# Attention output in token order: one store per output tile, the last product in two column halves, one product held back

## The chip, the cores and the metric

The kernel runs on one core of one Trainium2 chip. The metric is the device time of one execution in microseconds; the time of a kernel is the median of several executions.

## The reference

Softmax attention over 8 batches of 12 heads, 448 tokens and 64 dimensions per head, followed by a two-layer block with a SiLU between its layers. All tensors are float32.

```python
scores = np.matmul(q, k.transpose(0, 1, 3, 2)) / sqrt(64)     # q, k, v: (8, 12, 448, 64)
attn = softmax(scores)
attn_out = np.matmul(attn, v)
x = attn_out.transpose(0, 2, 1, 3).reshape(8 * 448, 12 * 64)  # (3584, 768)
h = x @ w_in                                                  # w_in:  (768, 2048)
g = h / (1 + np.exp(-h))
out = g @ w_out                                               # w_out: (2048, 768), out: (3584, 768)
```

## The kernel before

**Attention.** The work is cut into 24 units, one for each batch and group of four heads; a unit takes all 448 tokens. The queries of a unit are loaded so that partition 32 * head + i holds the 14 neighbouring tokens 14 * i to 14 * i + 13 (`group_of`, `TPP` is 14). After the 32 x 32 transposes (`turn_k`, `turn_q`) column 32 * g + i of a unit stands for token 14 * i + g. So the scores, their exponentials (`expo`, L442, on ScalarE), the products with V (`attend`, L479) and all that follows have their columns in the order "g i" and not in token order. Two exponentials of a unit are added on VectorE (`add_e`, L453) into T; sums of T and E over the keys are products with ones (L495, L515). `inverse` transposes the sums, takes the reciprocals (L554) and transposes them back (L546, L560) into `rdn`.

**The normalisation.** `norm` (L576) takes the product with V from a PSUM bank, multiplies it by 0.5 and by `rdn`, and writes one of the six 128 x 448 fp16 slices of `xT` of its batch. It runs twice per unit, 48 times in all. It frees the PSUM bank that the product stood in.

**The two layers.** The first layer (`ffn1`, L394, or `pair_product`, L729, for two batches together) multiplies slices of `w_in` by `xT` and leaves h / 2 in a PSUM bank. `tanh` (L602) and `gate` (L640), or ScalarE's SiLU (L755), make the gated values `G` (and `X` for columns that lie over), with the columns in the order of `xT`. The second layer works on "quads": two row tiles of 128 columns of G, and two halves of 384 output columns, done with seven products instead of eight by combining operands (`combine_g` makes the sums `S`, L779; `combine_w` the differences `D` of the weights, L627). A quad's products run in the order 1, 5, 6, 2, 7, 3, 4. Each is eight matmuls of 384 columns (`product`). Three PSUM banks serve a quad: products 1 and 2 add up in the first, 6, 7 and 4 in the second, 5 and 3 in the third. Between them VectorE adds copies of banks into banks (`add_in`, L840: "u", then "w", which products 7 and 3 wait for), and `add_out` (L845) and `take_out` (L836, on ScalarE) write the four 128 x 384 float32 output tiles `ost`, of which four buffers exist. There are 14 quads, 0 to 13.

**The stores.** Because the columns are in the order "g i", 32 neighbouring rows of an output tile are 32 rows of the output that stand 14 rows apart. `store` (L825) therefore sends each tile with four DMAs of 32 rows, all from SyncE (SP), but for the last two quads, where ScalarE (ACT) issues every second one.

**What sets the order.** The order of all instructions is written out by a planner inside the kernel. `Order` keeps an assumed clock and, for each engine, the operations that may run; each `Op` has an assumed duration, what it depends on and a bias. The planner gives `norm` the duration 448 / 960 + 0.13 us. `Ring` objects hand out the buffers and banks by their assumed times of release. Nothing of it runs on the chip: there every engine takes its instructions in the order that the planner wrote down, and waits on semaphores.

Of the kernel before, what the change touches and what calls it, by code (L numbers as in the profile page):

```python
# [17 lines left out]
PE_OUT = 0.20  # L18
# [12 lines left out]
def mm(n):  # L31
    return n / 2400.0 + 0.0026


def act(n):
    return n * 0.00087 + 0.13
# [151 lines left out]
def kernel(  # L188
# [9 lines left out]
    nc = tc.nc  # L198

    B, NH, S, D = q.shape  # L200
# [4 lines left out]
    TPP = S // 32  # L205
# [9 lines left out]
    NT = 2 * S // 128  # L215
    OH = DM // 2
# [33 lines left out]
    def bank_m(*key):  # L250
        return bank_of(4 + spot[key])
# [45 lines left out]
    rawk, rawq, KT, QT, E, T, acc, rdn_t, xT, g_t, ost_t = ({} for _ in range(11))  # L297
# [92 lines left out]
    def wide(out, lhsT, rhs, **flags):  # L390
        n = 4 if od.strips else 1
        for j in range(n):
            at = slice(128 // n * j, 128 // n * (j + 1))
            nc.tensor.matmul(out=out[at], lhsT=lhsT[:, at], rhs=rhs, **flags)  # L394
# [169 lines left out]
    def x3(b, cc):  # L564
        if (b, cc // 3) not in xT:
            xT[(b, cc // 3)] = sb.tile(
                [128, 3, S], FP16, name=f"xT_{b}_{cc // 3}", tag="xT", bufs=NX3
            )
        return xT[(b, cc // 3)]

    def norm(n, part):
        b, hg, g0, g1 = units[n]
        nq = 32 * (g1 - g0)
        cc = 2 * hg + part - 1
        x3(b, cc)
        nc.vector.scalar_tensor_tensor(  # L576
            out=x3(b, cc)[:, cc % 3, 32 * g0 : 32 * g1],
            in0=acc[(n, part)][:, 0:nq],
            scalar=0.5,
            in1=rdn_t[n].rearrange("p g i -> p (g i)"),  # L580
            op0=ALU.mult,
            op1=ALU.mult,
        )
# [25 lines left out]
    HF = NFF // 2  # L609
    G = const.tile([128, NFF, 2 * S], FP16, name="G")  # L610
    X = const.tile([128, NFF, 128], FP16, name="X")
    W_ = {m: const.tile([128, HF, OH], FP16, name=f"D{m}") for m in (5, 6, 4)}
# [36 lines left out]
    def rows(t, i):  # L649

        fs = slice(HF * i, HF * (i + 1))
        u, k = divmod(t, NT)
        if u % 2 == 0 and k == NT - 1:
            return X[:, fs]
        return G[:, fs, 128 * k : 128 * (k + 1)]
# [106 lines left out]
    S_t, tmp_t, ost_t, pr_t = {}, {}, {}, {}  # L762
# [17 lines left out]

    BANK = {1: 1, 2: 1, 6: 6, 7: 6, 4: 6, 5: 5, 3: 5}

    def product(qd, m, f0, f1):
        a, b = 2 * qd, 2 * qd + 1
        if m in (5, 6):
            w = S_t[(qd, m - 4)]
        else:
            t, i = {1: (a, 0), 2: (a, 1), 3: (a, 1), 7: (b, 0), 4: (b, 1)}[m]
            w = rows(t, i)
        if BANK[m] == m and f0 == 0:  # L790
            pr_t[(qd, m)] = bank_m("p", qd, m)
        for f in range(f0, f1):
            wide(
                out=pr_t[(qd, BANK[m])][:, 0:OH],
                lhsT=w[:, f, :],
                rhs=W_[m][:, f, :],
                start=(f == 0 and BANK[m] == m),
                stop=(f == HF - 1),
                skip_group_check=True,
            )  # L800


    def bank(qd, m):
        return pr_t[(qd, m)][:, 0:OH]
# [5 lines left out]
    def ost(qd, i, j):  # L810
        t = sb.tile([128, OH], FP32, name=f"ost_{qd}_{i}{j}", tag="ost", bufs=NOST)
        ost_t[(qd, i, j)] = t
        return t

    def store(qd, i, j):
        u, t = divmod(2 * qd + i, NT)
        for w in range(4):
            r, col = divmod(128 * t + 32 * w, S)
            b = 2 * u + r
            dst = out[b * S : (b + 1) * S, OH * j : OH * (j + 1)].rearrange(  # L820
                "(i g) m -> g i m", g=TPP
            )

            eng = nc.scalar if w % 2 and 4 * qd + 8 >= NT * B else nc.sync
            eng.dma_start(  # L825
                out=dst[col // 32], in_=ost_t[(qd, i, j)][32 * w : 32 * (w + 1), :]
            )

    def take(qd, m):
        nc.scalar.copy(out=tmp(qd, m), in_=bank(qd, m))  # L830

    def take_out(qd, m, i, j):
        if m == 6 and qd == NT * B // 4 - 1:
            nc.vector.tensor_copy(out=ost(qd, i, j), in_=bank(qd, m))
        else:
            nc.scalar.copy(out=ost(qd, i, j), in_=bank(qd, m))  # L836
        store(qd, i, j)

    def add_in(qd, to, x, y):
        nc.vector.tensor_tensor(  # L840
# [16 lines left out]
    units = []  # L857
# [5 lines left out]
    od = Order(SHY)  # L863
# [68 lines left out]
    for n in range(NB0 + NG, NU):  # L932
        b, hg = units[n][:2]
# [47 lines left out]
    pr_op, sg_op, w_op = {}, {}, {1: [], 2: [], 3: []}  # L981
# [5 lines left out]
    def in_parts(n, size, columns, emit, done, at=0):  # L987
        to = min(at + size, n)
        op = Op("PE", (to - at) * mm(columns), lambda: emit(at, to), tail=PE_OUT)
        od.on_pe(op, "full")  # L990
        if to == n:
            done(op)
        else:
            moe.insert(
                0, (list, 0, lambda: in_parts(n, size, columns, emit, done, to), ())
            )
# [264 lines left out]
    def queue_quad(qd):  # L1261
        quads.append(qd)
        fourth.append(qd)
        took = {}

        def read(name, eng, fn, deps, then=None):
            busy = act(OH) if eng == "ACT" else OH / 960.0 + 0.13
            bias = B_TAKE if eng == "ACT" else B_READ
            took[name] = od.add(Op(eng, busy, fn, deps, bias, then=then))

        def out(m):
            def then(at):
                m_ring.give(at, spot[("p", qd, m)])
                ost_ring.give(at + STORE)

            return then

        def queue(m):
            def run():
                if BANK[m] == m:  # L1280
                    spot[("p", qd, m)] = m_ring.take()[0]
                for ring, need in rings:
                    ring.take(need)
                in_parts(HF, PROD_AT, OH, lambda f0, f1: product(qd, m, f0, f1), done)

            def done(op):
                if m == 5:
                    sg_ring.give(od.free["PE"] + PE_OUT)
                pr_op[(qd, m)] = op
                if m in (1, 5):  # L1290
                    read(m, "ACT", lambda: take(qd, m), [op])
                elif m == 6:
                    read("u", "DVE", lambda: add_in(qd, 6, 6, 1), [op, took[1]], tmp_ring.give)
                    read("w", "DVE", lambda: add_in(qd, 5, 6, 5), [took["u"], took[5]])
                elif m == 2:
                    read("11", "ACT", lambda: take_out(qd, 1, 0, 0), [op], out(1))
                elif m == 7:
                    read(
                        "22",
                        "DVE",  # L1300
                        lambda: add_out(qd, 6, 5, 1, 1),
                        [op],
                        lambda at: (ost_ring.give(at + STORE), tmp_ring.give(at)),
                    )
                elif m == 3:
                    read("12", "ACT", lambda: take_out(qd, 5, 0, 1), [op], out(5))
                else:
                    eng = "DVE" if qd == NT * B // 4 - 1 else "ACT"
                    read("21", eng, lambda: take_out(qd, 6, 1, 0), [op], out(6))

            def deps():
                made = list(w_op.get(m, [None]))
                made += [took.get(x) for x in {2: (1,), 7: ("w",), 3: ("w",), 4: ("22",)}.get(m, ())]
                first = {5: 1, 6: 5, 7: 6, 3: 7, 4: 3}.get(m)
                if first:
                    made.append((pr_op.get((qd, first)), 9.0))
                elif m == 1 and qd > 0:
                    made.append((pr_op.get((qd - 1, 1)), 9.0))
                if m in (1, 2, 4):
                    t = 2 * qd + (m == 4)  # L1320
                    for b in {(128 * t + c) // S for c in (0, 127)}:
                        for f in range(HF):
                            x = g_op.get((b, f + HF * (m > 1)), [None])
                            made += [(y, f * mm(OH)) for y in x]
                    return made + ld_wout
                x = sg_op.get((qd, {5: 1, 6: 2, 7: 3, 3: 4}[m]), [])
                x = x if len(x) == 2 else [None, None]
                return made + [x[0], (x[1], 4 * mm(OH))]

            rings = ((tmp_ring, 1),) if m in (1, 5) else ((ost_ring, 1),) * (m != 6)  # L1330
            moe.append((deps, int(BANK[m] == m), run, rings))

        for m in (1, 5, 6, 2, 7, 3, 4):
            queue(m)
# [300 lines left out]
    while True:  # L1635
# [49 lines left out]
        if warm["on"] and at is not None and od.free["PE"] <= od.now and wait > 0.06 and od.now > 0.9:  # L1685
            each = mm(128) if od.now > COLD else 0.07 if od.now > 6.5 else 0.107
            n = max(1, int((wait - 0.06) / each), int(wait / each + 0.9) * (od.now < 14.0))
            n += MORE0 * (6.5 < od.now < COLD) + 2 * (COLD < od.now < 14.0)
            if warm.pop("first", None):
                n = FIRST  # L1690
# [36 lines left out]
```

## Time and profile before

| what | value |
|---|---|
| median of 3 runs | 382.66 us (382.15 to 384.31) |
| the profiled execution's own time | 382.59 us |
| its span in the profile | 380.5 us |
| granted TensorE clock | 0.998 |
| PE busy | 373.6 us, 98% |
| DVE busy | 280.1 us, 74% |
| ACT busy | 254.4 us, 67% |
| `norm`, L576 | 48 times, mean 616 ns |
| stores | 208 from SP, 16 from ACT, 48 KB each, median 1.6 us (SP) and 1.8 us (ACT) to landing |

The profile shows one execution. PE is TensorE's matmuls, PEld its weight loads, DVE VectorE, ACT ScalarE, POOL GpSimd, SP SyncE. "L576" is line 576 of the kernel. A group of instructions is listed with its output and inputs, its count, its busy time and the mean of one, and then the idle time of the engine just before them with what ended it. The chain of waits goes back from the last instruction through whatever released each step. All times in the views are microseconds from the start of the span, unless marked ns.

### The profile page before, as it was taken

The numbers are of one execution on the slowest core, as the hardware profiler recorded it, in microseconds if no ns is written. First come the engines' busy times: TensorE is split into PE (matmuls) and PEld (weight loads), VectorE is DVE, ScalarE is ACT, GpSimd is POOL, SyncE is SP. The second block draws the span as 40 slices with busy tenths as digits, with TensorE's granted clock in tenths as the row PEclk, the third lists the DMA queues.
The fourth block names the chain that finished last, engine by engine and source line by source line (L and its number), as shares of the span: only waits on it lengthen the run. The fifth ranks groups of instructions, "written<-read, shape, count | busy, mean of one in ns | idle before, by whom it ended". The sixth has DMA issues, their size and how long they took to land.

```text
span 380.5 us, 12915 instructions
## 1 busy us (share of the span) xinstructions
PE 373.6 (98%) x5508; PEld 191.6 (50%) x5508; DVE 280.1 (74%) x560; ACT 254.4 (67%) x408; POOL 85.2 (22%) x155
## 2 busy tenths in 40 slices
PE   7999999999999999999999999999999999999995
PEld 6433455444455444444444454555556555556563
DVE  4689799999996868997869978789866334556333
ACT  4998864787867787967788787728762258772221
POOL 7537616406042603324240500000000000000000
PEclk9999999999999999999999999999999999999999
DMA  6999999936558843739491612120002330001333
GB/s 102 195 207 181 191 210 205 155 73 90 70 102 134 146 67 42 107 72 167 82 150 26 92 24 73 33 55 0 1 2 68 84 98 2 0 1 39 104 93 99
DMA packets 36009, 34.66 MB, mean 91 GB/s; under 512 B 12144, under 2 KB 35184, under 8 KB 35952
## 3 DMA queue, kind: packets, MB, share of 16 engines
q0 software_dynamic: 25200, 22.82, 40.5%
q1 hardware_dynamic: 9984, 10.24, 10.0%
q10 hardware_dynamic: 768, 0.79, 0.8%
q8 instruction: 43, 0.70, 0.8%
q14 instruction: 14, 0.11, 0.1%
HBM read 45.61 MB, written 11.01 MB: 149 GB/s over the span
## 4 chain that ended last, share of the span: by engine, by line
PE 93%; ACT 2%; DMA 2%; DVE 1%; issue 1%; POOL 0%; ACTq 0%; DVEq 0%; POOLq 0%
PE banks L394 55%; PE banks L729 15%; PE banks L404 11%; PE banks L479 10%; ACT E L442 2%; PE banks L495 2%; DMA rq<-in_q_dram 1%; PE banks L1626 0%; DMA out_dram<-ost 0%; DVE banks L840 0%; POOL rk L309 0%; DVE T L453 0%; PE banks L515 0%; DVE rq L387 0%; DVE ost L845 0%
## 5 line engine op out<-in xcount | busy, mean ns | idle before, releaser
L442 ACT ACTIVATE E<-banks 128x896 f16<-128x896 f32 x168 | 144.1, 919 | 41.4 <-PE banks L404 41.1
L394 PE MATMUL banks<-xT,w_in_t 128*32 128x448 f16 (+1 forms) x1446 | 90.5, 353 | 0.0
L394 PE MATMUL banks<-w_out_t,G 128*32 128x384 f16 (+1 forms) x1000 | 72.8, 327 | 0.1
L394 PEld LDWEIGHTS <-G 128*32 128x32 f16 (+1 forms) x1280 | 50.8, 97 | 36.9 <-issue 6.8
L394 PEld LDWEIGHTS <-w_in_t 128*32 128x32 f16 (+1 forms) x1446 | 42.2, 97 | 43.2 <-issue 12.7
L340 POOL DMA_DIRECT2D V<-in_v_dram x84 | 46.0, 560 | 55.2 <-PE banks L479 42.9
L404 PE MATMUL banks<-rq,KT 32*128 32x448 f16 (+1 forms) x768 | 52.1, 362 | 1.6 <-DVE rq L387 1.3
L602 ACT ACTIVATE th<-banks 128x448 f16<-128x448 f32 x72 | 37.2, 553 | 15.0 <-PE banks L394 13.2
L640 DVE SCALAR_TENSOR_TENSOR G<-th,banks 128x448 f16<-128x448 f16 (+1 forms) x72 | 39.8, 571 | 4.9 <-ACT th L602 4.5
L836 ACT COPY ost<-banks 128x384 f32<-128x384 f32 x41 | 19.6, 482 | 33.7 <-PE banks L394 18.2
L394 PE MATMUL banks<-D,S 128*32 128x384 f16 (+1 forms) x560 | 40.9, 327 | 0.0
L479 PE MATMUL banks<-E,V 128*32 128x448 f16 x672 | 35.7, 353 | 0.0
L755 ACT ACTIVATE G<-banks 128x448 f16<-128x448 f32 (+1 forms) x56 | 29.1, 525 | 6.5 <-DVE banks L745 3.5
L576 DVE SCALAR_TENSOR_TENSOR xT<-banks,rdn 128x448 f16<-128x448 f32 x48 | 29.1, 616 | 5.4 <-PE banks L479 2.8
L394 PEld LDWEIGHTS <-S 128*32 128x32 f16 (+1 forms) x560 | 22.2, 97 | 15.7 <-issue 3.1
L745 DVE TENSOR_TENSOR banks<-banks,q 128x448 f32<-128x448 f32 x28 | 17.6, 632 | 16.6 <-PE banks L729 15.4
L404 PEld LDWEIGHTS <-KT 32*128 32x128 f16 (+1 forms) x768 | 12.5, 96 | 30.8 <-issue 27.4
L453 DVE TENSOR_TENSOR T<-E,E 128x1792 f16<-128x1792 f16 x22 | 23.7, 1078 | 5.6 <-ACT E L442 5.5
L453 DVE TENSOR_TENSOR T<-T,E 128x1792 f16<-128x1792 f16 x22 | 23.8, 1083 | 5.2 <-ACT E L442 5.2
L317 POOL DMA_DIRECT2D rq<-in_q_dram x25 | 14.0, 559 | 59.0 <-PE banks L404 48.0
L479 PEld LDWEIGHTS <-V 128*32 128x32 f16 x672 | 17.0, 97 | 16.0 <-issue 4.3
L729 PEld LDWEIGHTS <-w_in_t 128*128 128x128 f16 x168 | 16.4, 98 | 15.2
(150 smaller groups left out, 386.0 us busy)
## 6 DMA issues: line engine op xcount, KB each, us to landing
out_dram<-ost SPq DMA_DIRECT2D x208, 48.0 KB, 1.6
rk<-in_k_dram POOLq DMA_DIRECT2D x23, 224.0 KB, 5.3
rq<-in_q_dram POOLq DMA_DIRECT2D x23, 224.0 KB, 5.4
w_out_t<-in_moe_w_out_dram POOLq DMA_DIRECT2D x4, 768.0 KB, 12.9
V<-in_v_dram POOLq DMA_DIRECT2D x42, 64.0 KB, 4.2
V<-in_v_dram POOLq DMA_DIRECT2D x42, 48.0 KB, 4.5
w_in_t<-in_moe_w_in_dram POOLq DMA_DIRECT2D x3, 512.0 KB, 11.3
w_in_t<-in_moe_w_in_dram POOLq DMA_DIRECT2D x6, 256.0 KB, 6.3
```

The costliest lines, as they stand in the source:

```text
L340: nc.gpsimd.dma_start(out=v_of(b, hg0)[32 * x : 32 * (x + 1), at, 0:count, :], in_=v[b, hs].rearrange("h (i g) d -> i h g d", g=TPP)[:, :, ...
L394: nc.tensor.matmul(out=out[at], lhsT=lhsT[:, at], rhs=rhs, **flags)
L404: nc.tensor.matmul(out=pS[p0 : p0 + 32 * (x1 - x0), h % 2, at : at + nq], lhsT=KT[(b, hg)][32 * h : 32 * (h + 1), c, x0:x1, :, e], rhs=QT[ ...
L442: nc.scalar.activation(out=E[(n, w)][0:kr, 2 * y : 2 * y + 2, 0:nk], in_=pS_t[(n, w, y)][0:kr, :, 0:nk], func=AF.Exp, scale=attn_scale,)
L453: nc.vector.tensor_tensor(out=T[n], in0=T[n] if step else E[(n, 0)], in1=E[(n, step + 1)], op=ALU.add,)
L479: nc.tensor.matmul(out=a[32 * h : 32 * (h + 1), 0:nq], lhsT=w, rhs=e[k0:k1, h, at : at + nq], start=start, stop=stop,)
L576: nc.vector.scalar_tensor_tensor(out=x3(b, cc)[:, cc % 3, 32 * g0 : 32 * g1], in0=acc[(n, part)][:, 0:nq], scalar=0.5, in1=rdn_t[n].rearra ...
L602: nc.scalar.activation(out=th, in_=h_t[(b, f, t0)][:, 0 : t1 - t0], func=AF.Tanh)
L640: nc.vector.scalar_tensor_tensor(out=dst[:, f, at + lo : at + hi], in0=th_t[(b, f, t0)][:, lo - t0 : hi - t0], scalar=1.0, in1=h_t[(b, f, ...
L729: nc.tensor.matmul(out=pp_t[(f, PBANK[m])], lhsT=w[:, c, :], rhs=a[:, c, :], start=(c == 0 and m in (1, 6, 5)), stop=(c == 2), skip_group_ ...
L755: nc.scalar.activation(out=dst[:, f, at + lo : at + hi], in_=pp_t[(f % HF, x)][:, lo:hi], func=AF.Silu, scale=2.0,)
L836: nc.scalar.copy(out=ost(qd, i, j), in_=bank(qd, m))
```

## The change

- `norm` writes `xT` in token order: it reads the bank and `rdn` in the order "g i" as before, and writes the element of column 32 * g + i to column 14 * i + g. The elements are fp16, so that elements written one after the other lie 28 bytes apart. Nothing between `xT` and the output cares for the order of the columns.
- A tile of output is then 128 neighbouring rows, and `store` is one DMA of 128 rows x 384 columns, 192 KB, from SP.
- The very last product (quad 13, product 4) is made in two halves of 192 columns, eight matmuls each; DVE copies the first half out and SP stores it, ACT copies and stores the second.
- Quad 12's product 4 is held back until quad 13's product 6 has been queued.

```diff
     def norm(n, part):
-        b, hg, g0, g1 = units[n]
-        nq = 32 * (g1 - g0)
+        b, hg = units[n][:2]
         cc = 2 * hg + part - 1
         x3(b, cc)
         nc.vector.scalar_tensor_tensor(
-            out=x3(b, cc)[:, cc % 3, 32 * g0 : 32 * g1],
-            in0=acc[(n, part)][:, 0:nq],
+            out=x3(b, cc)[:, cc % 3].rearrange("p (i g) -> p g i", g=TPP),
+            in0=acc[(n, part)][:, 0:S].rearrange("p (g i) -> p g i", g=TPP),
             scalar=0.5,
-            in1=rdn_t[n].rearrange("p g i -> p (g i)"),
+            in1=rdn_t[n],
...
+    QL = NT * B // 4 - 1
+    OQ = OH // 2
+
-    def product(qd, m, f0, f1):
+    def product(qd, m, f0, f1, h=slice(0, OH)):
...
-                out=pr_t[(qd, BANK[m])][:, 0:OH],
+                out=pr_t[(qd, BANK[m])][:, h],
                 lhsT=w[:, f, :],
-                rhs=W_[m][:, f, :],
+                rhs=W_[m][:, f, h],
...
-    def store(qd, i, j):
-        u, t = divmod(2 * qd + i, NT)
-        for w in range(4):
-            r, col = divmod(128 * t + 32 * w, S)
-            b = 2 * u + r
-            dst = out[b * S : (b + 1) * S, OH * j : OH * (j + 1)].rearrange(
-                "(i g) m -> g i m", g=TPP
-            )
-
-            eng = nc.scalar if w % 2 and 4 * qd + 8 >= NT * B else nc.sync
-            eng.dma_start(
-                out=dst[col // 32], in_=ost_t[(qd, i, j)][32 * w : 32 * (w + 1), :]
-            )
+    def store(qd, i, j, h=slice(0, OH), eng=nc.sync):
+        row = 128 * (2 * qd + i)
+        eng.dma_start(
+            out=out[row : row + 128, OH * j : OH * (j + 1)][:, h],
+            in_=ost_t[(qd, i, j)][:, h],
+        )
...
     def take_out(qd, m, i, j):
-        if m == 6 and qd == NT * B // 4 - 1:
-            nc.vector.tensor_copy(out=ost(qd, i, j), in_=bank(qd, m))
+        nc.scalar.copy(out=ost(qd, i, j), in_=bank(qd, m))
+        store(qd, i, j)
+
+    def take_half(x):
+        h = slice(OQ * x, OQ * (x + 1))
+        t = ost_t.get((QL, 1, 0)) or ost(QL, 1, 0)
+        if x:
+            nc.scalar.copy(out=t[:, h], in_=bank(QL, 6)[:, h])
         else:
-            nc.scalar.copy(out=ost(qd, i, j), in_=bank(qd, m))
-        store(qd, i, j)
+            nc.vector.tensor_copy(out=t[:, h], in_=bank(QL, 6)[:, h])
+        store(QL, 1, 0, h, nc.scalar if x else nc.sync)
...
+                if qd == QL and m == 4:
+                    pr_op[(qd, m)] = None
+                    for x in range(2):
+                        h = slice(OQ * x, OQ * (x + 1))
+                        op = Op("PE", HF * mm(OQ), lambda h=h: product(qd, m, 0, HF, h), tail=PE_OUT)
+                        od.on_pe(op, "full")
+                        op.done += HF * mm(OQ) * x
+                        eng = "ACT" if x else "DVE"
+                        read(("21", x), eng, lambda x=x: take_half(x), [op])
+                    return
...
             def deps():
                 made = list(w_op.get(m, [None]))
...
+                if (qd, m) == (QL - 1, 4):
+                    made.append(pr_op.get((QL, 6)))
```

More of the change, by code (lines that the diff above doesn't have):

```diff
@@ L1307, in done @@
                 else:
-                    eng = "DVE" if qd == NT * B // 4 - 1 else "ACT"
-                    read("21", eng, lambda: take_out(qd, 6, 1, 0), [op], out(6))
+                    read("21", "ACT", lambda: take_out(qd, 6, 1, 0), [op], out(6))
             def deps():
```

## The prediction

> **What bounds the kernel now.** I read the page's busy table and slices first. Columns: engine, busy us, share of the span, instructions; then one digit per fortieth of the span.
>
> ```profile
> PE 373.6 (98%) x5508; PEld 191.6 (50%) x5508; DVE 280.1 (74%) x560; ACT 254.4 (67%) x408; POOL 85.2 (22%) x155
> PE   7999999999999999999999999999999999999995
> DVE  4689799999996868997869978789866334556333
> ```
>
> PE has no slack between its first and last slice; the change touches neither its columns nor their clock (granted 0.998). Time can only come from PE's two ends, and be lost where something makes PE wait. DVE, at 74% on average, runs at 8 to 9 tenths for the first two thirds, and all 48 normalisations (`norm`, L576) lie there, from 18.8 to 255 us.
>
> Next the costliest groups with shapes kept apart, for what one `norm` costs and what else tells of DVE's rate per element. Columns: operation, out<-in, count, busy us, mean ns.
>
> ```profile
> L640 DVE SCALAR_TENSOR_TENSOR G<-th,banks 128x448 f16<-128x448 f16 x52 | 30.3, 607 | 4.4 <-ACT th L602 4.2
> L576 DVE SCALAR_TENSOR_TENSOR xT<-banks,rdn 128x448 f16<-128x448 f32 x48 | 29.1, 616 | 5.4 <-PE banks L479 2.8 <-ACT E L442 1.0
> L640 DVE SCALAR_TENSOR_TENSOR X<-th,banks 128x128 f16<-128x128 f16 x20 | 5.5, 277 | 0.0
> L554 DVE RECIPROCAL inv<-sT 128x28 f32<-128x28 f32 x10 | 3.2, 318 | 0.1
> L554 DVE RECIPROCAL inv<-sT 128x14 f32<-128x14 f32 x4 | 1.0, 242 | 0.1
> ```
>
> L640 with 448 and with 128 neighbouring elements gives (607 - 277) / 320 = 1.03 ns per element. The reciprocal is the only DVE row whose elements are not neighbours: it reads words 64 or 128 bytes apart, and costs (318 - 242) / 14 = 5.4 ns per element, an unknown part of it the division.
>
> Then busy time by stretches around the ten bursts of four norms (from, to, length; PE, PEld, DVE busy). Three of them:
>
> ```profile
> 55.00:64.00 9.00, 9.00 (x208) 5.28 (x204) 8.58 (x20) 2.37 (x5) 3.90 (x8) 1.00 1.20 204
> 166.00:173.00 7.00, 7.00 (x156) 3.54 (x148) 6.66 (x15) 4.30 (x7) 3.22 (x6) 1.00 0.48 81
> 229.00:236.00 7.00, 7.00 (x148) 3.24 (x144) 6.90 (x13) 4.48 (x6) 0.00 (x0) 1.00 0.35 90
> ```
>
> DVE's idle time in them is 0.42, 0.34 and 0.10 us; over all ten, 73.0 - 67.05 = 5.95 us.
>
> Last the chain of waits at the end (start, us, what), for the tail:
>
> ```profile
> 342.47 28.61 PE banks L394 x176
> 371.18 0.58 DVE banks L840
> 371.85 0.58 DVE banks L840
> 372.47 1.47 PE banks L394 x8
> 373.96 0.57 DVE ost L845
> 374.97 1.60 DMA out_dram<-ost
> 376.57 0.55 DVE ost L834
> ```
>
> Only 371 to 377 is not plain PE: PE waits for quad 13's "w" (second L840), and the last copy (L834) is DVE's. The timeline has PE's last product, 1.46 us from 375.06, end at 376.52, so L834 waited for PE as much as for the store named.
>
> **The change part by part.** The instruction order of the changed program is the old one on every engine up to quad 12's last product, so all earlier effects come through durations.
>
> *Norm into token order.* Same 48 instructions, same elements read; each fp16 is now written 28 bytes behind the one before instead of 2. No row shows a DVE write with such a step. Low end: no cost, since L640, L576 and fp32 rows (L745, 448 elements to PSUM in 632 ns) all take about 1.03 ns per element whatever is written. High end: the reciprocal's 5.4 ns, (5.4 - 1.03) x 448 = +1.96 us per norm. Operation, type and source are L640's, so the value should lie near that end, but the step is what L640 lacks. I take one further DVE step per written element, 2.06 ns: **+0.46 us per norm, to about 1.08 us**, 22 us of DVE work in all. This is a choice, not a reading.
>
> The Trainium skill, "Vector Engine (DVE) Microarchitecture Reference", section 5.2 "Measured stream behaviour on trn2", speaks against this edit: a stream keeps its full rate only where neighbouring words come in pairs, and a destination that hops at every element takes 1.71 to 2.51 ns per column against 1.054. By it a norm would grow by some 0.30 to 0.65 us (an estimate from that page), and the sum below would be 383.2 to 391.5 us; no run so far shows it.
>
> What of that reaches PE? A burst's four norms add 4 x 0.46 = 1.84 us to a stretch with about 0.6 us of DVE idle. If nothing behind a burst gave way, PE would lose at most 18.4 - 5.95 = 12.5 us in the ten bursts, and some 2 us around the first eight norms (18.8 to 37 us). At least it loses what waits with no margin already. One such place, in the timeline:
>
> ```profile
> 168.14 0.62 DVE L576 SCALAR_TENSOR_TENSOR xT<-banks,rdn 128x448 f16<-128x448 f32 x1
> 168.68 0.63 DVE L387 STREAM_TRANSPOSE rq<-rq 128x448 f32<-128x448 f32 x1
> 169.58 0.62 DVE L576 SCALAR_TENSOR_TENSOR xT<-banks,rdn 128x448 f16<-128x448 f32 x1 [0.27 <-ACT E L442]
> 170.26 0.94 PE L479 MATMUL banks<-E,V 128*32 128x448 f16 x16
> ```
>
> The norm at 169.58 ends at 170.20 and PE starts at 170.26, one hop later: PE waits for the PSUM bank that this norm empties. Two longer norms lie on that chain, 0.92 us, less 0.15 to 0.27 of idle DVE between them (the wait and its hop): PE stops about 0.77 us. I followed every wait so, moving each instruction by the latest of what it waits for less the margin between their times. The stops: 22.1 to 25.9 us (bank of the first batch, three places) 0.72; 32.7 (sums waiting for T, L453) 0.32; 59.9 (first layer waiting for xT) 0.34; 63.9 (scores waiting for the q transpose behind the burst) 0.42; 97.9 (product waiting for S, behind a backlog from the burst at 87) 0.68; 110.3 (bank) 0.33; 170.3, 0.77; 251.4 and 255.7 (bank, xT) 0.25. Sum **3.8 us**; the other bursts have enough margin. The same addition gives 0.9 us for +0.30 per norm, 2.1 for +0.38, 9.2 for +0.65, about 60 for the +1.96 of the reciprocal's end.
>
> *One store per tile.* SP issues 56 instead of 208 at 0.42 us, ACT one instead of 16; SP does nothing else. A store had 9984 / 208 = 48 packets, three per DMA engine, of 0.100 x 16 x 380.5 / 9984 = 61 ns; it now has nine per engine, 0.55 us for 0.18. From copy to free slot: before 4 x 0.42 + 1.6 (median to landing) = 3.3, now 0.42 + 1.6 + 0.4 = 2.4 us. If issuing 128 rows took four times as long, 3.7. ACT waited 14.8 us for slots, but PE runs without a break from 342.47 to 371 beside it, so I take **0**. The bytes do not change.
>
> *One product held back.* Quad 12's product 4 goes behind quad 13's product 2, so that two products (2.6 us) instead of one (1.3) lie between product 6 and product 7, which needs "w". PE's 24 products from 370.91 take 4.15 us to the next line at 375.06, against 24 x 0.1625 = 3.90: **-0.25 us**. Its copy moves on ACT behind quad 13's first output, its store on SP likewise; nobody but the end waits for them.
>
> *Halves.* Eight matmuls of 384 columns become sixteen of 192, 81 ns each at the same rate. Eight more weight loads stay hidden: 25 zero matmuls, each with its 128x128 load, take 1.57 us (L1626 at 9.95), at most 63 ns a pair. But the order of the changed program with its waits shows no overlap: DVE's half waits for a PE signal that comes only after the second half, and ACT's half waits for DVE's. So after PE's end: DVE 0.557 - 192 x 1.03 ns = 0.36, ACT 0.478 - 192 x 0.8 (L742, 448 in 531) = 0.32, with hops 0.76, then one issue; before, 0.60 and two ACT issues, the second at 377.57, 1.05 behind PE. That is -0.3, and six more packets per engine give up to 0.37 back: **0**, from -0.3 to +0.4; +1.3 if the issue takes four times 0.42.
>
> Sum, on the profiled execution's own 382.59 us (span 380.5; the median of the runs, 382.66, is the same): +3.8 - 0.25 = **386.1 us**.
>
> **The rivals.** A change under 0.5%, 1.9 us, can't be told from none here.
>
> *Forecast*, +0.39 us or more per norm: 384.6 to 391.5, likeliest 386.1. For it: the only DVE row with hops is five times slower per element, and waits without margin exist. Against: that row also divides.
>
> *Not slower, because the write port takes any address at one element a step.* Norms stay at 616 ns (up to some 0.75 us, which the margins eat), only the tail is left: 382.3. For: L640 and L745 write different memories and types at one rate. It decides if a norm gains under 0.15 us.
>
> *Longer norms, swallowed by margins.* +0.15 to +0.39 each: PE loses 0 to 2.2 us, 382.3 to 384.5, likeliest 383.2. For: at +0.30 eight of the ten bursts cost PE nothing.
>
> The Trainium skill's "SBUF — State Buffer", section "Door 1", says without a figure that at least two hits on a 16-byte line are needed for full bandwidth; a step of 28 bytes gives one, and by that rule alone the norms grow, by the forecast or by this rival; no row here shows it.
>
> *The stores become the bound.* If issuing 128 rows takes 1.7 us, the end comes 1.3 later: 383.6 with unchanged norms. Against: one descriptor row costs 61 ns of sixteen engines.
>
> **How the numbers follow.** Forecast 0.55, unchanged norms 0.21, swallowed 0.19, stores 0.02. A gain over 1.9 us has 0.03: after PE's end there are only 4.0 us, most of it landing and closing. So faster 0.03, same 0.42, slower 0.55. The range runs from 382.0, just under the unchanged norms, to 390.5, norms at some +0.62; the forecast's own is 384.6 to 390.5. The reciprocal's end is left out, as I give it under 0.05.
>
> **What would show it.** In the new profile: the mean of the norm group (1.08 us forecast; 0.62 and 0.9 the rivals), DVE's busy time (302 against 280), PE idle at the places listed, the pitch of quad 13's products without the 0.25 us hole, and the last copy on ACT starting where DVE's ends. A norm mean under 0.95 us makes the forecast wrong; a mean of 1.08 with a time under 384.6 makes the addition of margins wrong.

## Result: 431.3 us against 382.5

The changed kernel took 431.29 us (median of 4 runs, 429.84 to 431.86), the kernel before 382.51 us beside it (382.15 to 384.31): a ratio of 1.126, with an interval of 1.121 to 1.130. The prediction was 386.1 us with a range of 382.0 to 390.5. "Slower" was right, by the mechanism it named (longer norms for which PE waits), and the size was wrong by a factor of nearly fourteen: 48.8 us where 3.55 were forecast.

The profiled execution took 431.31 us with a span of 429.5. Its busy table and slices, read like those of before:

```profile
PE 386.2 (90%) x5516; PEld 196.0 (46%) x5516; DVE 345.4 (80%) x560; ACT 256.0 (60%) x409; POOL 85.3 (20%) x155
PE   8967896999788989887998979898899999999996
DVE  5799899999999998999898997999886733547432
```

PE lost its unbroken row of nines over nearly three quarters of the span, where the norms are, and nowhere else. DVE's busy time is up by 65.3 us, while its average is still only 80%: an average over the whole span does not show that DVE is full in the stage where the norms are.

The groups (operation, count, busy us and mean ns, then idle before and its releaser), the new line of `norm` and of the gate that serves as its yardstick:

```profile
L575 DVE SCALAR_TENSOR_TENSOR xT<-banks,rdn 128x448 f16<-128x448 f32 x48 | 99.4, 2204 | 2.2 <-PE banks L479 1.8
L639 DVE SCALAR_TENSOR_TENSOR G<-th,banks 128x448 f16<-128x448 f16 x52 | 30.9, 620 | 2.0 <-ACT th L601 1.9
```

The gate stayed where it was (607 before); a norm went from 616 to 2204 ns, +1.59 us, which is (2204 - 616) / 448 = 3.5 ns more for each element written. The prediction took +0.46.

The waits (engine, its line, whom it waited for: us in all, times, longest) have two entries of PE that the kernel before lacks. They are the two uses of `norm` that the prediction followed: it fills `xT` for the first layer, and it frees the PSUM bank for the next product with V.

```profile
PE banks L394 <- DVE xT L575: 14.3, 20, 2.0
PE banks L479 <- DVE xT L575: 12.3, 13, 1.4
```

The burst that the prediction quoted, its norm at 169.58 in the trace of before, is this in the timeline of after (that norm, and PE's two stops there):

```profile
199.53 2.09 DVE L575 SCALAR_TENSOR_TENSOR xT<-banks,rdn 128x448 f16<-128x448 f32 x1
...
199.22 0.94 PE L479 MATMUL banks<-E,V 128*32 128x448 f16 x16 [0.85 <-DVE xT L575]
...
201.68 0.94 PE L479 MATMUL banks<-E,V 128*32 128x448 f16 x16 [1.35 <-DVE xT L575]
```

The norm ends at 201.62 and PE starts at 201.68, by the same wait and the same 0.06 us as before: 1.35 us of idle PE at a place for which 0.77 was forecast.

The burst ahead of it had margin enough in the prediction's addition (its norms start at 147.94 to 150.83 in the trace of before) and shows how that margin is used up; PE's rows first, then DVE's:

```profile
175.21 1.70 PE L479 MATMUL banks<-E,V 128*32 128x448 f16 x32 [0.86 <-DVE xT L575]
...
179.69 0.94 PE L394 MATMUL banks<-xT,w_in_t 128*32 128x448 f16 x16 [0.64 <-DVE xT L575]
...
184.53 0.83 PE L394 MATMUL banks<-w_out_t,X 128*32 128x384 f16 x16 [1.56 <-DVE G L639]
```

```profile
173.03 2.12 DVE L575 SCALAR_TENSOR_TENSOR xT<-banks,rdn 128x448 f16<-128x448 f32 x1 [0.32 <-PE banks L479]
174.78 0.82 DVE L639 SCALAR_TENSOR_TENSOR G<-th,banks 128x448 f16<-128x448 f16 x1
175.53 6.08 DVE L575 SCALAR_TENSOR_TENSOR xT<-banks,rdn 128x448 f16<-128x448 f32 x3
```

DVE holds four norms in a row with one gate between them, and PE stops three times, 3.06 us in all: for the bank, for `xT`, and at 184.53 for a gate that stood in DVE's queue behind the burst. The chain of waits agrees, by shares of the span, before and after ("issue" is time in which an engine waited for nothing that the profile shows; a name with q is an engine's sequencer):

```profile
PE 93%; ACT 2%; DMA 2%; DVE 1%; issue 1%; POOL 0%; ACTq 0%; DVEq 0%; POOLq 0%
PE 64%; DVE 28%; issue 3%; DMA 3%; POOL 1%; ACT 0%; DVEq 0%; POOLq 0%
```

Of the 49.0 us by which the span grew, 36.4 are PE's idle time (6.9 before, 43.3 after). The other 12.6 stand in PE's busy time, for the same work. Some 7 of them are the stops again: the record of a group of matmuls runs on for about 0.16 us after the next group could start (in `e4_hold` below, sixteen matmuls stand as 2.76 us and the next start 2.60 after them), so that much of a stop counts as busy, and at 47 places PE stops longer than in the same program with dense norms (`e2_dense`). Some 5 are the clock, which the prediction took as untouched: from 72.4, 256.8 and 304.5 us it was granted at half for 3.4 us each, which costs 5.1 us, and so does 0.988 over the whole span, (1 - 0.988) x 429.5. The four runs of the changed kernel were granted 0.980 to 0.992; the kernel before had 0.998. What brought the half clock on was not tested.

### The profile page after: what moved, and what is told of

Same layout as the page of the kernel before. It is cut to its first block, busy times and chain, and to the rows that moved or that the text cites. A ratio compares the mean times of both kernels' runs of the same rounds, so it can differ in the third digit from the quotient of the medians.

```text
span 429.5 us, 12684 instructions
## 1 busy us (share of the span) xinstructions
PE 386.2 (90%) x5516; PEld 196.0 (46%) x5516; DVE 345.4 (80%) x560; ACT 256.0 (60%) x409; POOL 85.3 (20%) x155
## 4 chain that ended last, share of the span: by engine, by line
PE 64%; DVE 28%; issue 3%; DMA 3%; POOL 1%; ACT 0%; DVEq 0%; POOLq 0%
PE banks L394 41%; DVE xT L575 19%; PE banks L728 13%; PE banks L404 6%; DMA rk<-in_k_dram 3%; DVE T L453 3%; PE banks L479 2%; DVE G L639 2%; PE banks L495 1%; DVE KT L377 1%; DVE rq L387 1%; DVE rdn L560 0%; DVE S L778 0%; DVE G L778 0%; DVE sT L546 0%
## 5 line engine op out<-in xcount | busy, mean ns | idle before, releaser
L394 PE MATMUL banks<-xT,w_in_t 128*32 128x448 f16 (+1 forms) x1446 | 93.8, 354 | 13.0 <-DVE xT L575 12.5
L575 DVE SCALAR_TENSOR_TENSOR xT<-banks,rdn 128x448 f16<-128x448 f32 x48 | 99.4, 2204 | 2.2 <-PE banks L479 1.8
L394 PE MATMUL banks<-w_out_t,G 128*32 128x384 f16 (+1 forms) x1000 | 75.7, 338 | 3.8 <-DVE G L639 2.8
L394 PEld LDWEIGHTS <-G 128*32 128x32 f16 (+1 forms) x1288 | 52.8, 99 | 42.4 <-issue 8.4
L479 PE MATMUL banks<-E,V 128*32 128x448 f16 x672 | 36.8, 353 | 8.9 <-DVE xT L575 8.8
L639 DVE SCALAR_TENSOR_TENSOR G<-th,banks 128x448 f16<-128x448 f16 (+1 forms) x72 | 41.0, 588 | 2.3 <-ACT th L601 1.9
L404 PEld LDWEIGHTS <-KT 32*128 32x128 f16 (+1 forms) x768 | 12.6, 96 | 32.6 <-issue 27.1
```

Source lines behind the costliest of these rows:

```text
L404: nc.tensor.matmul(out=pS[p0 : p0 + 32 * (x1 - x0), h % 2, at : at + nq], lhsT=KT[(b, hg)][32 * h : 32 * (h + 1), c, x0:x1, :, e], rhs=QT[ ...
L479: nc.tensor.matmul(out=a[32 * h : 32 * (h + 1), 0:nq], lhsT=w, rhs=e[k0:k1, h, at : at + nq], start=start, stop=stop,)
L575: nc.vector.scalar_tensor_tensor(out=x3(b, cc)[:, cc % 3].rearrange("p (i g) -> p g i", g=TPP), in0=acc[(n, part)][:, 0:S].rearrange("p (g ...
L639: nc.vector.scalar_tensor_tensor(out=dst[:, f, at + lo : at + hi], in0=th_t[(b, f, t0)][:, lo - t0 : hi - t0], scalar=1.0, in1=h_t[(b, f, ...
```

## The experiments

The theory after the result: a write that hops costs several ns per element on its own, and all of the loss is the length of `norm`. Rivals: the cost comes from the three-dimensional pattern whatever its step; from DVE being disturbed by the other engines at the same memory; from the stepped reads; or part of the loss is in the stores, the halves or the held product.

**One instruction by itself (`e1_steps`).** A program of its own that does none of the reference's work: `norm`'s instruction six times each with 448 elements, the patterns of output and inputs varied, then a copy by ScalarE in the same way, with no other compute engine at work. (DMAs of zeros to the output ran for its first 31 us, beside the rows for dense fp16 and for steps of up to 14 bytes.)

```diff
+    for _ in range(6):      # e.g. lone fp16 elements 28 bytes apart
+        nc.vector.scalar_tensor_tensor(out=h.rearrange("p (i g) -> p g i", g=14), in0=a0, ...)
```

> A kernel of its own that does none of the reference's work: VectorE alone repeats the normalisation's operation (PSUM and SBUF float32 in) six times for each of several access patterns, then ScalarE a copy. Theory: what costs is the byte distance between elements written one after the other. Then the dense fp16 row takes about 0.6 us, the 28-byte step about 2.1 us as in the changed kernel's fastest norm, steps up to 8 bytes cost little, and float32 at 28 bytes costs as much as fp16 at 28 bytes. Rival 1, the pattern of 14 x 32 elements itself costs: then the step of 4 bytes takes 2.1 us too. Rival 2, writing half of a 4-byte word costs (two writes in one): then float32 stays at 0.6 us at every step and fp16 is slow from 4 bytes on. Rival 3, contention with the other engines: then the 28-byte step takes about 0.6 to 1.1 us here, where nothing else runs.

From the groups of its profile, fp16 output with the dense output as the first line, then steps of 4, 8, 16 and 28 bytes, and pairs of neighbours 28 bytes apart:

```profile
L74 DVE SCALAR_TENSOR_TENSOR h<-banks,rdn 128x448 f16<-128x448 f32 x6 | 3.7, 614 | 0.2
L77 DVE SCALAR_TENSOR_TENSOR h<-banks,rdn 128x448 f16<-128x448 f32 x6 | 3.9, 654 | 0.2
L80 DVE SCALAR_TENSOR_TENSOR h<-banks,rdn 128x448 f16<-128x448 f32 x6 | 6.9, 1149 | 0.2
L86 DVE SCALAR_TENSOR_TENSOR h<-banks,rdn 128x448 f16<-128x448 f32 x6 | 12.8, 2133 | 0.2
L89 DVE SCALAR_TENSOR_TENSOR h<-banks,rdn 128x448 f16<-128x448 f32 x6 | 12.5, 2077 | 0.2
L131 DVE SCALAR_TENSOR_TENSOR hb<-banks,rdn 128x448 f16<-128x448 f32 x6 | 3.8, 626 | 0.2
```

float32 output with steps of 8, 16 and 28 bytes; then fp16 written densely, reading PSUM at a step of 128 bytes, and SBUF float32 at such a step; then ScalarE copying PSUM to fp16, dense and at 28 bytes:

```profile
L104 DVE SCALAR_TENSOR_TENSOR f<-banks,rdn 128x448 f32<-128x448 f32 x6 | 3.7, 625 | 0.2
L107 DVE SCALAR_TENSOR_TENSOR f<-banks,rdn 128x448 f32<-128x448 f32 x6 | 5.7, 946 | 0.2
L110 DVE SCALAR_TENSOR_TENSOR f<-banks,rdn 128x448 f32<-128x448 f32 x6 | 5.7, 957 | 0.2
L143 DVE SCALAR_TENSOR_TENSOR h<-banks,rdn 128x448 f16<-128x448 f32 x6 | 3.7, 624 | 0.2
L146 DVE SCALAR_TENSOR_TENSOR h<-banks,rdn 128x448 f16<-128x448 f32 x6 | 5.4, 902 | 0.2
L152 ACT CAST h<-banks 128x448 f16<-128x448 f32 x6 | 3.2, 532 | 0.2
L155 ACT CAST h<-banks 128x448 f16<-128x448 f32 x6 | 12.4, 2072 | 0.2
```

The change's own pattern takes 2077 ns with nothing else running, against 2204 in the kernel: disturbance is at most 0.13 us of the 1.59. The pattern's third dimension costs next to nothing (654 at a step of 4 bytes), and so does a PSUM read with a step (624); a step in the read from SBUF costs 0.29 us (902). What costs is the written element: a lone fp16 element, half of a 4-byte word, costs the full price from a step of 16 bytes on, and at 8 bytes a third of the increase (535 of some 1500 ns); 448 float32 words at 28 bytes take 957, and pairs of fp16 neighbours no more than dense output. Of what was expected, the 2.1 us at 28 bytes came out; but float32 words do not cost as much as lone fp16 elements, and a step of 8 bytes is not cheap. The rival of the half words is not right as it stood either: by it float32 would have stayed at 0.6 us and fp16 been slow from 4 bytes on. One reading fits all the rows of writes: with 0.15 us fixed, each visit to another stretch of 16 bytes costs (2133 - 150) / 448 = 4.4 ns if a half word is written there and (946 - 150) / 448 = 1.8 ns if whole words are, but the instruction never takes less than the dense 0.61 to 0.66 us. At 8 bytes, where every second element opens a new stretch, that gives 224 x 4.4 + 150 = 1136 ns for 1149 measured. The fit is a description of the table; why a half word costs more was not tested. ScalarE pays nearly the same time (2072), so this is no trait of DVE's datapath alone.

**The changed kernel with the dense norm (`e2_dense`).** Everything else of the change stays; each batch's rows come out in another order.

```diff
-            out=x3(b, cc)[:, cc % 3].rearrange("p (i g) -> p g i", g=TPP),
-            in0=acc[(n, part)][:, 0:S].rearrange("p (g i) -> p g i", g=TPP),
-            in1=rdn_t[n],
+            out=x3(b, cc)[:, cc % 3],
+            in0=acc[(n, part)][:, 0:S],
+            in1=rdn_t[n].rearrange("p g i -> p (g i)"),
```

> The changed kernel with the old dense norm, so that the rows of each batch come out in another order; stores, halves and the product held back stay. Theory: the norm alone costs the 49 us, the rest is worth -0.25 us: 382.3 us, norm 0.62 us, no hole of 0.25 us in quad 13's products. Rival, the stores of 192 KB or the halves cost part of it: 385 us or more, with ACT or DVE waiting longer for stores.

382.11 us (381.63 to 383.30, 11 runs) against 382.40: ratio 0.9994 (0.9985 to 1.0004). Stores, halves and held product together can't be told from nothing. Its timeline at the end:

```profile
374.50 1.48 PE L394 MATMUL banks<-D,G 128*128 128x192 f16 x16
...
376.08 0.36 DVE L837 COPY ost<-banks 128x192 f32<-128x192 f32 x1 [2.12 <-PE banks L394]
376.47 0.32 ACT L835 COPY ost<-banks 128x192 f32<-128x192 f32 x1 [1.25 <-DVE ost L837]
376.82 0.38 ACTq L819 DMA_DIRECT2D out_dram<-ost  x1
```

PE works the sixteen matmuls of the two halves without a gap, DVE's copy starts only 0.10 us after PE's last end at 375.98, and ScalarE's starts after DVE's: the two halves follow one another, as the order of the instructions had shown.

**The norm alone (`e3_norm_alone`).** The kernel before, with only `norm` in the new form; its stores then send rows to wrong places.

```diff
-            out=x3(b, cc)[:, cc % 3, 32 * g0 : 32 * g1],
-            in0=acc[(n, part)][:, 0:nq],
-            in1=rdn_t[n].rearrange("p g i -> p (g i)"),
+            out=x3(b, cc)[:, cc % 3].rearrange("p (i g) -> p g i", g=TPP),
+            in0=acc[(n, part)][:, 0:S].rearrange("p (g i) -> p g i", g=TPP),
+            in1=rdn_t[n],
```

> The kernel before with only the norm's write in token order; stores and tail as before, so that rows come out in a wrong place. Theory: 431.5 us (431.3 plus the 0.25 that the tail's edits gave), norm 2.2 us. Rival, stores or tail cost part of the 49 us: 427 us or less.

432.65 us (432.13 to 434.10) against 382.40: ratio 1.131 (1.129 to 1.133).

```profile
L576 DVE SCALAR_TENSOR_TENSOR xT<-banks,rdn 128x448 f16<-128x448 f32 x48 | 99.6, 2201 | 2.6 <-PE banks L479 2.1
```

One edited instruction gives the whole loss, at the same mean. With the run before it, the loss is settled from both sides.

**The held product alone (`e4_hold`).** The kernel before with this line.

```diff
+                if (qd, m) == (NT * B // 4 - 2, 4):
+                    made.append(pr_op.get((qd + 1, 6)))
```

> The kernel before with only quad 12's product 4 held back behind quad 13's product 6. Theory: the hole of 0.25 us ahead of quad 13's product 7 closes, 382.3 us against 382.55, hardly to be told from no change by its time, so the trace decides: 24 products in 3.9 us instead of 4.15. Rival, another wait takes its place (a bank or an output buffer): the hole moves behind another product and the time stays or rises.

382.39 us against 382.40: ratio 1.000 (0.9991 to 1.0009). In the timeline the hole is closed:

```profile
370.48 1.46 PE L394 MATMUL banks<-D,G 128*128 128x384 f16 x8
371.78 2.76 PE L394 MATMUL banks<-w_out_t,G 128*128 128x384 f16 x16
374.38 1.46 PE L394 MATMUL banks<-D,G 128*128 128x384 f16 x8
```

24 matmuls (three products; the prediction calls the matmuls products here) take 374.38 - 370.48 = 3.90 us, as worked out, instead of 4.15. A quarter of a microsecond is smaller than what eleven runs resolve here (0.34), so its worth in time is neither shown nor excluded.

**The changed kernel with a step of 8 bytes (`e5_step8`).** The same instruction writes another order of columns, with a growth per norm near the one that the prediction had assumed; each batch's rows come out in another order.

```diff
-            out=x3(b, cc)[:, cc % 3].rearrange("p (i g) -> p g i", g=TPP),
+            out=x3(b, cc)[:, cc % 3].rearrange("p (i g) -> p g i", g=4),
```

(and both inputs likewise)

> The changed kernel with the norm's elements written 8 bytes apart instead of 28 (another order of the columns, so that output rows come out in other places). It puts the norm near the length that the prediction assumed. Theory: the addition of margins was right and only the norm's length wrong. Alone on VectorE this form took 1.15 us; with the 0.05 to 0.15 us that norms gain beside the other engines the group's mean is 1.15 to 1.25, +0.53 to +0.63 us each, and the margins give +5.3 to +8.5 us on the 382.1 of the same kernel with dense norms: 387.4 to 390.6 us. Rival, the margins mislead: PE loses the whole overflow of the bursts (14 us or more: 396 us or more) or nearly nothing (384 us or less).

```profile
L575 DVE SCALAR_TENSOR_TENSOR xT<-banks,rdn 128x448 f16<-128x448 f32 x48 | 53.4, 1180 | 2.7 <-PE banks L479 2.0
```

387.19 us (387.00 to 387.57) against 382.70: ratio 1.011 (1.008 to 1.014), 0.2 under the lower end of what was expected. A growth of 0.56 us per norm costs some 4.5 us, where the prediction had 3.8 for +0.46 and 9.2 for +0.65: what it had wrong is the growth, and not the way the margins were added.

The places agree too. `e5_step8` and `e2_dense` have the same 5516 matmuls in the same order, so that PE's delay can be read matmul by matmul. In times of the trace of before, and counting delays over 0.1 us from 12 us on, PE loses 0.64 us in all at 22.1 to 25.9, 0.67 at 32.7, 0.22 at 56.9, 0.57 at 59.9, 0.49 at 63.9, 0.53 at 97.9, 0.46 at 108.1, 0.53 at 170.3 and 1.01 at 251.4 and 255.7. That is the prediction's list of stops, but that 56.9 is new and the stop at 110.3 came at 108.1.

**Hops in the reads (`e6_read`) and in the transpose (`e7_turned`).** Both keep the token order and all the rest of the change, and write `xT` densely. The first reads the bank and `rdn` with a step of 128 bytes; the second has the 24 transposes that make `rdn` write it in token order, as float32 words 56 bytes apart, so that `norm` reads only PSUM with a step.

```diff
-            out=x3(b, cc)[:, cc % 3].rearrange("p (i g) -> p g i", g=TPP),
-            in0=acc[(n, part)][:, 0:S].rearrange("p (g i) -> p g i", g=TPP),
-            in1=rdn_t[n],
+            out=x3(b, cc)[:, cc % 3].rearrange("p (i g) -> p i g", g=TPP),
+            in0=acc[(n, part)][:, 0:S].rearrange("p (g i) -> p i g", g=TPP),
+            in1=rdn_t[n].rearrange("p g i -> p i g"),   # e6; e7: in1=rdn_t[n], and
+            #  rdn_t[n] is [128, 32, 14], transposed into .rearrange("p i g -> p g i")
```

> The changed kernel with the same result, but the norm reads its two inputs in token order (PSUM and SBUF 128 bytes apart) and writes neighbours. Theory: the write was the cost; alone on VectorE this form took 0.90 us, +0.28, of which the margins let 0.6 to 0.9 us reach PE: 382.8 us, the same as before within 0.5%. Rival, the reads get slower beside PE and ScalarE, which use the same memories: norm over 1.05 us and 385 us or more.

> The changed kernel with the same result, but the 24 transposes that make the norm's factors write them in token order (float32 words 56 bytes apart), so that the norm reads only PSUM with a step and writes neighbours. Theory: norm 0.62 us as before; the transposes go from 0.63 to about 0.93 us if they pay as the float32 writes at 56 bytes did; the margins let 0.35 us through: 382.4 us, as the kernel with dense norms within 0.1%. Rival, a transpose with a step pays more than a product: 1.1 us or more each and 383.4 us or more.

The groups, the first line from `e6_read`:

```profile
L575 DVE SCALAR_TENSOR_TENSOR xT<-banks,rdn 128x448 f16<-128x448 f32 x48 | 43.7, 939 | 2.7 <-PE banks L479 2.3
```

and from `e7_turned`:

```profile
L575 DVE SCALAR_TENSOR_TENSOR xT<-banks,rdn 128x448 f16<-128x448 f32 x48 | 28.8, 613 | 2.4 <-ACT E L442 0.7 <-PE banks L479 0.6
...
L560 DVE STREAM_TRANSPOSE rdn<-inv 128x448 f32<-128x448 f32 x24 | 21.4, 953 | 0.4
```

`e6_read` took 384.18 us (383.79 to 384.93, 12 runs) against 382.70, ratio 1.0037 (1.0026 to 1.0049): 1.4 us over what was expected of it, with norms of 0.94 us where 0.90 were expected. `e7_turned` took 382.90 (382.47 to 383.43, 12 runs), ratio 1.0003 (0.9991 to 1.0015), where 382.4 was expected: the change's idea at no cost that these runs resolve, as 24 transposes grow by 0.33 us instead of 48 norms by 1.59. It does not beat the kernel before either. No run did; what token order was to bring, one store per tile, is worth nothing here.

## Why the prediction was wrong

**The step that failed** is the size of "*Norm into token order*": "I take one further DVE step per written element, 2.06 ns: +0.46 us per norm". Measured: +1.59, by `e3_norm_alone` in the kernel, and 2077 - 614 = 1463 ns, +1.46, by `e1_steps` alone; a lone fp16 element takes 4.6 ns in all (2077 / 448). No row of the trace showed a DVE write with such a step, as the prediction says itself, and it chose a value near the low end of its bound because operation, type and source were L640's, "but the step is what L640 lacks".

That the measured +1.59 lies inside the bound of 0 to +1.96 is luck. The high end came from the reciprocal, but by the kernel that instruction hops in what it reads and writes neighbours, and its elements are float32. A read of float32 in SBUF at a step of 128 bytes took 902 ns against 614 in `e1_steps`, 0.6 ns more per element, where the reciprocal lay 4.4 above L640: most of its price is something else (the division, presumably; not tested). It was no measure of a write.

**The second failure follows from the first.** The text itself gave the price of the high end, "about 60 for the +1.96 of the reciprocal's end", and left it out of the range as under 0.05 likely. No row of the trace supported so small a chance. So the range stopped short of a bound at the one term that mattered.

Two smaller readings were off without changing the sum: DVE's slices show 6 to 9 tenths in the first two thirds and not 8 to 9, and the "24 products" of the last quad are matmuls.

The Trainium skill had given a number for a write that hops: in "Vector Engine (DVE) Microarchitecture Reference", section 5.2 "Measured stream behaviour on trn2 (trn3 not measured)", a hopping destination takes 1.71 to 2.51 ns per column. The float32 rows of `e1_steps` agree (946 to 957 ns for 448, 2.1 ns each, or 1.8 without the fixed 0.15 us); the fp16 rows do not (2077 to 2133, 4.6 to 4.8). The section's programs write 4-byte words, and the prediction carried its figure over to half words; the choice of +0.46 lies inside what it worked out from it, +0.30 to +0.65.

The Trainium skill's "SBUF — State Buffer", section "Door 1", asks for at least two hits on a 16-byte line. By the runs that holds for float32 (625 ns at a step of 8 bytes, 946 at 16) and not for lone fp16 elements, which have two hits at a step of 8 bytes and take 1149.

**The addition of margins held** roughly in the sum, and in the places (`e5_step8`). The prediction's own figures, joined by straight lines (an estimate), against each run's distance from the changed kernel with the dense norm (ratios of one group of runs to the kernel before beside it, times 382.5):

| growth per norm, us | addition | measured |
|---|---|---|
| 0.32 (`e6_read`) | 1.2 (0.9 for +0.30, 2.1 for +0.38) | 1.6 |
| 0.56 (`e5_step8`) | 6.6 (3.8 for +0.46, 9.2 for +0.65) | 4.6 |
| 1.59 (the change) | 46 (9.2 for +0.65, about 60 for +1.96) | 48.4 |

In the last row some 5 of the 48.4 are the half clock, which the addition does not count. Most of a small growth is swallowed: 15.5 us of longer DVE work (48 x 0.32) came through as 1.6. Of a further growth from 0.56 to 1.59, 49 us of DVE work, 44 came through.

**One store per tile: 0**, held. A store of 128 rows lands after 1.9 us (median) for 1.6, ScalarE's waits for slots, 14.8 us before, are gone from the list, and the time did not move (`e2_dense`).

```profile
out_dram<-ost SPq DMA_DIRECT2D x55, 192.0 KB, 1.9
```

The rival "the stores become the bound" rested on an issue of 1.7 us; SP's issues of 128 rows took 0.33 us (median of 56 in the changed kernel), ScalarE's one 0.38 in the view above.

**Product held back: -0.25** held in the trace (3.90 us), and is not measurable in the time. **Halves: 0** held, for the reason given: the copies run one after the other.

**The rivals.** "The write port takes any address at one element a step" fell (2077 ns on an idle core). "Swallowed by margins" fell for this change, though `e6_read` came out as that rival has it. DVE's busy time, forecast at 302, was 345.4. The conditions that the prediction named for being wrong did not include this one: a mean far over 1.08.

## What to carry to other kernels

Count a stepped write by its element's size and its step: an fp16 element alone in its 16 bytes took 4.5 to 4.8 ns here (steps of 16 to 64 bytes), a float32 word about 2, and a pair of fp16 neighbours no more than dense output. If an order must be turned, put the hops where they are free or rare: in a read from PSUM, or in a float32 tile made once for several uses. And where no row of the trace has the feature in question, time the instruction by itself first, as `e1_steps` did, or let the range reach both ends of the bound: a row of another operation that hops elsewhere prices something else.

## What had not been expected of the hardware

- VectorE and ScalarE take the same 2.07 us to write 448 lone fp16 elements 28 bytes apart, though their dense rates differ (614 and 532 ns).
- PSUM is read at a step of 128 bytes at full rate by both (624 ns for 614, and 532 for 532), while SBUF read so costs VectorE 902, float32 or fp16 (899).
- A stream transpose with its output words 56 bytes apart takes 953 ns instead of 626.
